# Talking-heads attention and squared-ReLU FFN: the first batch's triple matrices, loads and w_out are rearranged

## The chip, the cores and the metric

The kernel runs on one core of a Trainium2 chip. The core has a matrix engine (TensorE, PE in the profile; PEld is its weight load), three engines for elementwise work (VectorE = DVE, ScalarE = ACT, GpSimd = POOL), SyncE (SP), which here only issues DMAs, and 16 DMA engines that all queues share. Loads from memory are issued by POOL and go through one queue (the page's q0); copies inside the core and stores are issued by SP and go through another (q1). The metric is the device time of one execution in microseconds.

## The reference

```python
scores = scale * np.matmul(q, k.transpose(0, 1, 3, 2))        # 8 batches, 12 heads, 448 x 448, head_dim 64
scores = np.einsum('bhij,hg->bgij', scores, w_pre)            # mix over the heads
scores = scores - np.max(scores, axis=-1, keepdims=True)
attn = np.exp(scores)
attn = attn / (np.sum(attn, axis=-1, keepdims=True) + 1e-09)
attn = np.einsum('bhij,hg->bgij', attn, w_post)               # mix over the heads again
attn_out = np.matmul(attn, v)
x = attn_out.transpose(0, 2, 1, 3).reshape(3584, 768)
h = np.maximum(x @ w_in, 0.0)                                 # w_in 768 x 2048
out = h * h @ w_out                                           # w_out 2048 x 768
```

Inputs and output are float32; inside, the kernel works in bfloat16 with float32 sums.

## The kernel before, in words

**One batch.** k and q are loaded with a cast to bfloat16 and transposed: for the first two batches on PE (L481), later by DMA transposes that SP issues (L557, L563), after POOL or DVE has copied them into place (L544). The 448 query rows of a head are 128 x 3 = 384 rows in three blocks (r = 1, 2, 3) and a tail of 64 rows (r = 0), for which the q of two heads are laid side by side (qt, transposed into zt). `score` (L607) makes the scores of a block, one matmul a head (L619), and DVE or ACT copies them into snat, one of two buffers, rows on partitions (L385 for DVE, L387 for ACT).

**Relayout.** The mixing over heads needs heads on partitions. `relayout` (L654) therefore copies pieces of snat by DMA into a tile sch of 120 partitions (10 query rows x 12 heads) and 448 keys; there are 11 such buffers. A batch has 45 such chunks. `move` (L647) issues the DMA on SP (L648). A buffer of snat may be written again when all relayouts that read it have landed.

**Chunk.** `chunk` does, for each piece: mixing by w_pre on PE (L743), minimum on DVE (L748, mn; the sign is turned), exponential with its sum on ACT (L751, es), reciprocal on DVE (L757, rc), the product with w_post on POOL (L760, wq), the second mixing on PE (L767), and a copy on DVE or ACT into atb (L385, L387). Six of these can be under way. `av` multiplies atb by v (L807) into xt.

**The first batch's triples.** In the first batch, the tail (r = 0) and the first block (r = 1) are moved by six large relayouts instead, of 120 rows x 1,344 elements: each serves three chunks, and such a chunk is made by three matmuls (L739) with masked copies of the mixing matrix. These 18 matrices of 120 x 120 are in one tile, wtri_all. `spread` (L429) makes six products of 120 x 120 on PE, three to a bank (L431); `thin` (L435) writes each of them three times, masked by a column of keep_m, on DVE (L438) or ACT (L440): 18 evictions. The relayouts' targets are osb (three times) and h2 (three times, "h" in the profile).

**FFN.** `unit` takes 128 or 256 rows of xt through w_in (L860), ReLU on ACT (L873, hr), the square on POOL (L876, h), w_out (L892), a copy on DVE (L907, osb) and a store (L916).

**Loads.** The first batch's k, q and tails are loaded at the start. Behind them POOL issues three pieces of w_in, two halves of v, and the other three pieces of w_in (`first_batch`, L1007; `load_w1`, `load_v`). The four pieces of w_out (`load_w2`, L982) are issued at steps 18, 21, 24 and 27 of the first batch, each 512 rows of w_out by all 768 columns. The loads of the second batch are issued at steps 13 and 16.

**What sets the order.** All instructions are written into fixed orders by a planner, a small list scheduler that runs when the kernel is built (`Planner.run`, L117). Every operation has an engine (or two to choose from), a duration and a priority (mostly the number of the chunk, with an offset such as AHEAD = 7 chunks for relayouts and scores). DMAs are modelled as two queues, LOAD and DMA, with a cost per row alone and a cost when both are active (`moved`, `settle`). The planner's durations only choose orders; on the chip an instruction waits for semaphores, and on each engine the order is kept.

## Time and profile before

| | us |
|---|---|
| median of 3 runs (597.18 to 598.89) | 597.46 |
| profiled execution, whole time | 597.42 |
| profiled execution, span | 595.6 |
| PE busy, 95% of the span | 565.2 |
| DVE busy, 81% | 484.6 |
| ACT busy, 80% | 475.9 |
| POOL busy, 55% | 325.0 |

The page's second part shows the span in 40 equal slices, each digit the busy share of a slice in tenths. In the timeline a row gives an instruction's start and duration, its engine, line, what it writes and reads, and in brackets how long the engine was idle before it and who ended that. Merged rows carry a count (x6). A row of the stretches gives, for PE, PEld, DVE, ACT and POOL, the busy time and the count of instructions, then the granted share of PE's clock, the mean busy share of the DMA engines (it can pass 1 where packets overlap) and the GB/s moved.

### The profile page before, as it was taken

The page shows a single profiled execution, that of the slowest core. Times are in us where ns is not written, and L with a number is a line of the kernel's source. Part 1 is how long each engine was busy: PE and PEld are TensorE (multiplying, and loading weights), DVE is VectorE, ACT ScalarE, POOL GpSimd, SP SyncE. Part 2 cuts the span into 40 slices and gives each one's busy share as a digit, 9 for nine tenths or more (in the row PEclk, how much of TensorE's full clock was granted, in tenths as well). Part 3 has the DMA queues.
Part 4 walks back from the last instruction along what each step waited for, and adds up shares of the span by engine and source line. Part 5 has one row for each costly group of instructions (what it writes and reads, how often), then busy time and mean ns, then how long its engine had stood idle before and what let it go on. Part 6 is the DMA issues. An engine that isn't in the chain of part 4 may idle for free.

```text
span 595.6 us, 17018 instructions
## 1 busy us (share of the span) xinstructions
PE 565.2 (95%) x5751; PEld 402.4 (68%) x5751; DVE 484.6 (81%) x1248; ACT 475.9 (80%) x1246; POOL 325.0 (55%) x596
## 2 busy tenths in 40 slices
PE   4687978999999999999999999999999999999996
PEld 2345765587667766776866868776867767777873
DVE  5699958989989898999799998989799998888011
ACT  4488967898888898998898978888888888998420
POOL 8026635564567637753784728653884726445530
PEclk9799999999999999999999999999999999999999
DMA  9959963986499647974399649884398646322011
GB/s 136 234 125 175 220 144 83 197 177 146 103 162 177 151 120 136 187 172 135 94 179 173 157 114 164 173 146 133 87 191 165 150 116 126 119 82 69 2 53 54
DMA packets 130038, 82.33 MB, mean 138 GB/s; under 512 B 59582, under 2 KB 124238, under 8 KB 129950
## 3 DMA queue, kind: packets, MB, share of 16 engines
q1 hardware_dynamic: 85214, 58.42, 38.7%
q0 software_dynamic: 44736, 22.81, 29.4%
q8 instruction: 45, 0.74, 0.5%
q14 instruction: 43, 0.35, 0.2%
HBM read 45.62 MB, written 11.01 MB: 95 GB/s over the span
## 4 chain that ended last, share of the span: by engine, by line
PE 84%; DVE 6%; DMA 4%; issue 2%; ACT 2%; POOL 1%; SPq 0%; DVEq 0%; ACTq 0%; POOLq 0%
PE bank L892 24%; PE bank L860 24%; PE bank L767 12%; PE bank L743 11%; PE bank L807 6%; PE bank L619 6%; DVE mn L748 2%; DMA sch<-snat 2%; DVE atb L385 1%; DMA osb<-snat 1%; DVE snat L385 1%; PE bank L739 1%; DMA ks<-in_k_dram 1%; ACT es L751 1%; DVE rc L757 1%
## 5 line engine op out<-in xcount | busy, mean ns | idle before, releaser
L751 ACT ACTIVATE es<-bank,mn 120x448 bf16<-120x448 f32 x360 | 229.5, 644 | 37.0 <-DVE mn L748 27.3
L760 POOL TENSOR_SCALAR wq<-wback,rc 120x120 bf16<-120x120 f32 x360 | 132.2, 371 | 196.5 <-DVE rc L757 113.9
L748 DVE TENSOR_REDUCE mn<-bank 120x1 f32<-120x448 f32 x360 | 210.2, 609 | 7.8 <-PE bank L739 5.3
L892 PE MATMUL bank<-w,h 128*128 128x384 bf16 x896 | 173.9, 325 | 0.6 <-DVE osb L907 0.3
L860 PE MATMUL bank<-xt,w 128*128 128x256 bf16 (+1 forms) x1632 | 165.5, 255 | 0.0
L385 DVE CAST atb<-bank 112x480 bf16<-112x480 f32 (+2 forms) x222 | 135.1, 620 | 23.5 <-PE bank L767 21.3
L860 PEld LDWEIGHTS <-w 128*128 128x128 bf16 x1632 | 137.3, 98 | 22.5 <-issue 2.0
L876 POOL TENSOR_TENSOR h<-hr 128x512 bf16<-128x512 f32 x112 | 116.6, 1041 | 57.3 <-ACT hr L873 57.1
L767 PEld LDWEIGHTS <-es 120*112 120x112 bf16 (+1 forms) x1440 | 113.2, 130 | 41.1 <-issue 11.3
L767 PE MATMUL bank<-wq,es 120*112 120x120 bf16 (+1 forms) x1440 | 124.9, 217 | 7.6 <-POOL wq L760 5.9
L892 PEld LDWEIGHTS <-h 128*128 128x128 bf16 x896 | 84.0, 97 | 54.8 <-issue 4.9
L385 DVE CAST snat<-bank 128x448 bf16<-128x448 f32 x170 | 98.8, 611 | 11.9 <-DMA sch<-snat 5.3
L743 PE MATMUL bank<-sch,wmix 120*128 120x448 bf16 x334 | 105.3, 354 | 0.1
L387 ACT CAST atb<-bank 112x480 bf16<-112x480 f32 (+2 forms) x162 | 88.2, 555 | 11.4 <-PE bank L767 10.5
L873 ACT ACTIVATE hr<-bank 128x512 f32<-128x512 f32 x112 | 67.0, 599 | 33.3 <-PE bank L860 28.9
L387 ACT CAST snat<-bank 128x448 bf16<-128x448 f32 x166 | 82.7, 546 | 11.2 <-DMA sch<-snat 4.4
L751 ACT ACTIVATION_READ_ACCUMULATOR es<-bank,mn 120x1 f32 x360 | 75.8, 211 | 0.0
L757 DVE RECIPROCAL rc<-sm 120x1 f32<-120x1 f32 x360 | 52.9, 153 | 20.3 <-ACT es L751 16.6
L907 DVE COPY osb<-bank 128x384 f32<-128x384 f32 x56 | 30.9, 551 | 35.9 <-PE bank L892 35.8
L619 PE MATMUL bank<-kt,qz 64*128 64x448 bf16 x288 | 43.3, 359 | 4.9 <-DVE snat L385 3.8
L743 PEld LDWEIGHTS <-wmix 120*128 120x128 bf16 x342 | 29.9, 98 | 18.6 <-issue 11.1
L807 PE MATMUL bank<-atb,vs 112*64 112x192 bf16 (+3 forms) x864 | 40.4, 250 | 0.2
(56 smaller groups left out, 250.8 us busy)
## 6 DMA issues: line engine op xcount, KB each, us to landing
sch<-snat SPq DMA_DIRECT2D x318, 105.0 KB
out_dram<-osb SPq DMA_DIRECT2D x23, 360.0 KB
vs<-in_v_dram POOLq DMA_DIRECT2D x16, 336.0 KB, 9.4
ks<-in_k_dram POOLq DMA_DIRECT2D x14, 336.0 KB, 7.0
qs<-in_q_dram POOLq DMA_DIRECT2D x14, 288.0 KB, 7.1
w<-in_moe_w_in_dram POOLq DMA_DIRECT2D x6, 512.0 KB, 14.7
w<-in_moe_w_out_dram POOLq DMA_DIRECT2D x4, 768.0 KB, 19.7
out_dram<-osb SPq DMA_DIRECT2D x8, 192.0 KB
```

The source lines that it names most:

```text
L385: nc.vector.tensor_copy(out=out_, in_=in_)
L387: nc.scalar.copy(out=out_, in_=in_)
L619: nc.tensor.matmul(slot[:, 0:S], lhsT=lhsT, rhs=kt[i][half, :, at_, :], start=True, stop=True)
L743: nc.tensor.matmul(slot[:, 0:S], lhsT=wm[0:rows, :], rhs=src[0:rows, :], start=True, stop=True,)
L748: nc.vector.tensor_reduce(out=mn[i][0:rows, :], in_=slots[mk][0:rows, 0:S], axis=AX.X, op=ALU.min)
L751: nc.scalar.activation(out=es[i][0:rows, 0:S], in_=slots[mk][0:rows, 0:S], func=ACT.Exp, scale=-1.0, bias=mn[i][0:rows, 0:1], accum_out=sm ...
L760: nc.gpsimd.tensor_scalar(out=wq[i][0:rows, :, 0:ns], in0=wback[0:rows, :, 0:ns], scalar1=rc[i][0:rows, 0:1], scalar2=1.0, op0=ALU.mult, o ...
L767: nc.tensor.matmul(slot[0:P_KEYS, jb * H * ns:(jb + 1) * H * ns], lhsT=es[i][0:rows, jb * P_KEYS:(jb + 1) * P_KEYS], rhs=wq[i][0:rows, :, ...
L807: nc.tensor.matmul(v_[64 * hh:64 * hh + 64, i, 0:x1 - x0], lhsT=vs[:, 2 * c2 + hh, jb, :], rhs=atb[half][:, jb, 2 * c2 + hh, x0:x1], start ...
L860: nc.tensor.matmul(slot[:, j * w:(j + 1) * w], lhsT=w1[c2][:, (f0 + j) * 128:(f0 + j + 1) * 128], rhs=xt[:, c2, a:z], start=(c2 == 0), sto ...
L876: nc.gpsimd.tensor_tensor(out=h2_[:, f0:f0 + nf, 0:w], in0=hr[gi % 2][:, :].rearrange("p (f c) -> p f c", f=nf), in1=hr[gi % 2][:, :].rear ...
L892: nc.tensor.matmul(slot[:, 0:384], lhsT=h2_[:, ft, mt * 128:(mt + 1) * 128], rhs=w2[:, ft, nt * 384:(nt + 1) * 384], start=(ft == 0), stop ...
```

## The change

- The evictions into wtri_all take three products at a time (120 x 3 x 120): six instructions instead of 18.
- v and w_in of the first batch are loaded behind a small copy on POOL (hold), which reads snat after all scores of the first batch's tail have been copied there; v comes first, then the six pieces of w_in.
- A piece of w_out is now 1,024 rows by half of the columns (384) instead of 512 rows by all 768. Size, number and steps of the loads stay.
- In the planner, a relayout that finds its queue empty while a load is in progress is held until up to 50 rows of loads have passed (FIFO); the loads' costs alone and beside other traffic are set apart, with new numbers (also for q, k and the tails, in `first`, `load_tails` and `load_ahead`); AHEAD goes from 7 to 7.4. This emits no instruction and changes orders.

```diff
-AHEAD = 7
+AHEAD = 7.4
+FIFO = 50
@@ class Queue
+        self.last, self.wait = -1, -1
@@ Planner.run
                 if eng in queues:
                     x = queues[eng]
+                    y = queues["LOAD"]
+                    if eng == "DMA" and x.op is None and heap and y.op is not None and x.last != t and x.wait < t:
+                        ahead = max(0.0, y.left - (t - y.at) * y.rate) + sum(z[2].rows[0] for z in ready["LOAD"])
+                        x.wait = t + int(min(ahead, FIFO) * y.op.rows[1])
+                        heapq.heappush(events, (x.wait, n, None))
+                        n += 1
+                    if eng == "DMA" and x.wait > t:
+                        continue
...
@@ load
-        done = pl.moved("LOAD", rows, each, each, 0, [op], 1500)
+        done = pl.moved("LOAD", rows, each[0], each[1], 0, [op], 1500)
@@ thin
-    def thin(eng, tail, m, x):
-        src, to = slots["g", "tri", tail][0:KC, x * KC:(x + 1) * KC], wtri[3 * tail + m][x][:, 0:KC]
+    def thin(eng, tail, m):
+        src = slots["g", "tri", tail][0:KC, 0:3 * KC].rearrange("p (x k) -> p x k", x=3)
+        to = wtri_all[:, 9 * tail + 3 * m:9 * tail + 3 * m + 3, 0:KC]
...
         for m in range(3):
-            for x in range(3):
-                thins.append(add(
-                    {"DVE": 220, "ACT": 300}, 0, at_pri + 0.1 * m, lambda eng, tail=tail, m=m, x=x: thin(eng, tail, m, x), [mm],
-                ))
-                tri_ready.setdefault(3 * tail + m, []).append(thins[-1])
+            thins.append(add(
+                {"DVE": 500, "ACT": 560}, 0, at_pri + 0.1 * m, lambda eng, tail=tail, m=m: thin(eng, tail, m), [mm],
+            ))
+            tri_ready.setdefault(3 * tail + m, []).append(thins[-1])
@@ load_w1, load_w2, load_half
-        w1_in.append(load(16, 173, pri, lambda: nc.gpsimd.dma_start(
+        w1_in.append(load(16, (152, 148), pri, lambda: nc.gpsimd.dma_start(
...
     def load_w2(f4, n):
-        done = load(32, 135, n, lambda: nc.gpsimd.dma_start(
-            out=w2[:, 4 * f4:4 * f4 + 4, :],
-            in_=moe_w_out[512 * f4:512 * f4 + 512, 0:DMODEL].rearrange("(f p) c -> p f c", p=128),
+        f_, c_ = 8 * (f4 % 2), 384 * (f4 // 2)
+        done = load(64, (62, 79), n, lambda: nc.gpsimd.dma_start(
+            out=w2[:, f_:f_ + 8, c_:c_ + 384],
+            in_=moe_w_out[128 * f_:128 * f_ + 1024, c_:c_ + 384].rearrange("(f p) c -> p f c", p=128),
         ), gate(n))
...
+    def load_half(b, n, x, deps):
+        h0 = x * H // 2
+        v_in[b].append(load(42, (46, 58), n, lambda: load_kv(vs, v, b, h0, h0 + H // 2), deps))
@@ load_v
-        v_in[b] = [load(42, 60, n, lambda h0=h0: load_kv(vs, v, b, h0, h0 + H // 2), deps) for h0 in (0, H // 2)]
+        v_in[b] = [load(42, (46, 58), n, lambda h0=h0: load_kv(vs, v, b, h0, h0 + H // 2), deps) for h0 in (0, H // 2)]
...
@@ first_batch
         for i in range(NPAIR):
-            if i == LAST_W1:
-                load_v(0, 0.1 + i, [started])
-            load_w1(i, 0.1 + i)
...
         for r in (1, 0):
             for p in groups(0, r):
                 score(0, r, p)
+        hold = sb.tile([P, NPAIR], BF16, name="hold")
+        opened = add("POOL", 150, -6, lambda: nc.gpsimd.tensor_copy(
+            out=hold[:, :], in_=store_of(0, 0)[:, 0:NPAIR, 0],
+        ), scopy[0, 0])
+        for x in range(0, 2):
+            load_half(0, -5 + 0.1 * x, x, [opened])
+        for i in range(NPAIR):
+            load_w1(i, -4 + 0.1 * i, [opened])
```

More of the change, by code (lines that the diff above doesn't have):

```diff
@@ L75 @@
 Q1_AT = [13, 16]
-LAST_W1 = 3
+LAST_W1 = 4
 TAIL0, Q0 = 19, 0.7
@@ L234, in run @@
                         done.ns = t - done.at
-                        x.op = None
+                        x.op, x.last = None, t
                         x.turn += 1
@@ L946, in first @@
     def first(us, rows, each):
-        return pl.moved("LOAD", rows, each, each, 0, [add("FIRST", 0, us, lambda: None, lat=1000 * us + 1600)], 1500)
+        return pl.moved("LOAD", rows, each, each, 0, [add("FIRST", 0, us, lambda: None, lat=1000 * us + 1600)], 1300)
     at_, tails0 = 1.3, []
@@ L951 @@
         if what == "k":
-            k_in[0, x] = first(at_, 28, 60)
+            k_in[0, x] = first(at_, 28, 48)
         elif what == "q":
-            q_in[0, x] = first(at_, 32, 52)
+            q_in[0, x] = first(at_, 32, 36)
         else:
-            tails0.append(first(at_, 24, 32))
+            tails0.append(first(at_, 24, 24))
         at_ += 1.1 if at_ < 2 else 0.75
@@ L975, with load_w1 @@
     w2_in = [add("W2", 0, 0, lambda: None, lat=0) for i in range(4)]
-    def load_w1(c2, pri):
-        w1_in.append(load(16, 173, pri, lambda: nc.gpsimd.dma_start(
+    def load_w1(c2, pri, more=()):
+        w1_in.append(load(16, (152, 148), pri, lambda: nc.gpsimd.dma_start(
             out=w1[c2][:, :], in_=moe_w_in[c2 * 128:(c2 + 1) * 128, 0:DFF], max_dma_last_dim=4096,
-        ), [started]))
+        ), [started, *more]))
     def load_w2(f4, n):
-        done = load(32, 135, n, lambda: nc.gpsimd.dma_start(
-            out=w2[:, 4 * f4:4 * f4 + 4, :],
-            in_=moe_w_out[512 * f4:512 * f4 + 512, 0:DMODEL].rearrange("(f p) c -> p f c", p=128),
+        f_, c_ = 8 * (f4 % 2), 384 * (f4 // 2)
+        done = load(64, (62, 79), n, lambda: nc.gpsimd.dma_start(
+            out=w2[:, f_:f_ + 8, c_:c_ + 384],
+            in_=moe_w_out[128 * f_:128 * f_ + 1024, c_:c_ + 384].rearrange("(f p) c -> p f c", p=128),
         ), gate(n))
@@ L988, in load_w2 @@
         w2_in[f4].left += 1
+    def load_half(b, n, x, deps):
+        h0 = x * H // 2
+        v_in[b].append(load(42, (46, 58), n, lambda: load_kv(vs, v, b, h0, h0 + H // 2), deps))
     def load_v(b, n, deps):
-        v_in[b] = [load(42, 60, n, lambda h0=h0: load_kv(vs, v, b, h0, h0 + H // 2), deps) for h0 in (0, H // 2)]
+        v_in[b] = [load(42, (46, 58), n, lambda h0=h0: load_kv(vs, v, b, h0, h0 + H // 2), deps) for h0 in (0, H // 2)]
     def load_tails(b, n, deps):
-        tails = [load(24, 32, n, lambda x=x: load_tail(b, x), deps) for x in range(2)]
+        tails = [load(24, (24, 32), n, lambda x=x: load_tail(b, x), deps) for x in range(2)]
         tail_in[b] = add("TAIL", 0, n, lambda: None, tails, lat=1000 if b else 0)
@@ L999, in load_ahead @@
         got = [
-            load(48, 52, n, lambda: load_q(b, g0, g0 + 6), wars + gate(n)),
-            load(42, 60, n, lambda: load_kv(ks, k, b, g0, g0 + 6), wars + gate(n)),
+            load(48, (36, 52), n, lambda: load_q(b, g0, g0 + 6), wars + gate(n)),
+            load(42, (46, 58), n, lambda: load_kv(ks, k, b, g0, g0 + 6), wars + gate(n)),
         ]
@@ L1008, in first_batch @@
         for i in range(NPAIR):
-            if i == LAST_W1:
-                load_v(0, 0.1 + i, [started])
-            load_w1(i, 0.1 + i)
+            if i == 0:
+                v_in[0] = []
+                for x in range(0):
+                    load_half(0, -30 + x, x, [started])
         for p in range(NPAIR):
```

## The prediction

> **What bounds the kernel now.** I read the page first: busy shares, then the rows of 40 slices (one slice is 14.9 us).
>
> ```profile
> span 595.6 us, 17018 instructions
> ...
> PE   4687978999999999999999999999999999999996
> ...
> DVE  5699958989989898999799998989799998888011
> ...
> PEclk9799999999999999999999999999999999999999
> DMA  9959963986499647974399649884398646322011
> ```
>
> From slice 8 on PE is full. Adding up the gaps between PE's instructions gives 25.8 us of idle PE, 24.3 of them before 100 us (5.5 before the first matmul) and 1.5 after. Whatever is saved before 100 us moves the end one for one; what comes later can hardly be sped up.
>
> Then the timeline of the first 60 us, which shows the first hole and what stands before it. Columns: start, duration, engine, line, what, and in brackets the idle time and who ended it.
>
> ```profile
> 7.41 0.34 DVE L438 TENSOR_SCALAR wtri_all<-bank,keep_m 120x120 bf16<-120x120 f32 x1 [0.35 <-ACT wtri_all L440]
> 7.78 0.36 ACT L440 ACTIVATE wtri_all<-bank,keep_m 120x120 bf16<-120x120 f32 x1 [0.41 <-DVE wtri_all L438]
> ...
> 17.31 1.82 SPq L648 DMA_DIRECT2D osb<-snat  x2
> ...
> 21.84 2.66 SPq L648 DMA_DIRECT2D h<-snat  x3
> 24.44 5.22 PE L739 MATMUL bank<-osb,wtri_all 120*128 120x448 bf16 x15 [3.73 <-DMA osb<-snat]
> ```
>
> The 18 evictions into wtri_all take turns on DVE and ACT, each waiting for the other. The first triple relayout is issued at 17.31, and PE stands still until 24.44. Then the timeline of 74 to 92 us, the second hole:
>
> ```profile
> 85.52 1.16 DVE L385 CAST snat<-bank 128x448 bf16<-128x448 f32 x2 [4.82 <-DMA sch<-snat]
> 86.20 0.88 PE L619 MATMUL bank<-kt,qz 64*128 64x448 bf16 x4 [3.27 <-DVE snat L385]
> ...
> 87.82 2.75 PE L860 MATMUL bank<-xt,w 128*128 128x128 bf16 x24
> ```
>
> DVE and ACT are free from 80.7, but may not overwrite snat until the last relayout of the first batch has read it. Last, stretches of 2 us (busy time and count of PE, PEld, DVE, ACT, POOL; granted clock, DMA share, GB/s):
>
> ```profile
> 22.00:24.00 2.00, 0.00 (x0) 0.00 (x0) 0.00 (x0) 0.00 (x0) 0.00 (x0) 0.54 1.18 292
> 24.00:26.00 2.00, 1.56 (x5) 0.65 (x5) 0.24 (x1) 0.00 (x0) 0.00 (x0) 0.50 1.25 233
> ```
>
> After each hole PE runs at half clock: 6.83 us from 22.16, and 3.41 us from 87.02.
>
> The trace's DMA packets tell why the holes are there; loads go in the software queue, relayouts in SP's, on the same 16 engines. (a) osb's 2,688-byte packets start at 21.60, 4.3 us after the issue; a relayout into idle queues (schl, issued 42.74) starts after 1.4. In the missing 2.9 us about 50 packets of loads per engine go by (42 of v, the rest w_in). So a relayout that finds its own queue empty and loads ahead waits behind some 50 of these. (b) From 65 to 83.5 us every relayout of 120 packets takes 2.05 us (1.95 to 2.1), though all that count were issued by 69.4. The rate of w_out fits ten engines that take one 1,536-byte and one 896-byte packet in turn: 12 pairs of 171 ns.
>
> **The change, part by part.** The sum is against the profiled execution, 597.42 us (span 595.6); the median of the runs is 597.46.
>
> Evictions. 18 of 120 columns (ten at about 0.30 to 0.34 on DVE, eight at 0.36 on ACT: 6.1 us, taking turns from 7.0 to 14.2) become six of 360 columns. Not in the trace; between 0.34 (120 columns) and 0.61 (448) on DVE, 0.36 and 0.55 on ACT, by columns 0.53 and 0.50. The planned order gives DVE three in a row, then ACT three: 3.1 us and one handover. What this frees comes from the new order of PE: 7.67 start of the tails' transposes, 0.8; two zt copies on ACT to 9.2; then score 0.4, spread 0.5, k transposes 1.0, score 0.4, k transposes 1.0, two scores 0.7, q transposes 0.85, two scores 0.7, copy 0.6 = 15.3, less overlap of about 0.3: the six tails' copies are done at 15.0, against 17.2.
>
> Loads. The tensor_copy to hold on POOL (bounds: 0.10 for a 128x1 memset, 0.61 for a 112x512 copy; I take 0.2, near the 0.25 of the 120x144 memset) waits for those copies at 15.0; behind it on POOL stand 2 issues of v (0.78) and 6 of w_in (0.73) = 5.9 us, to 21.1, then the first wq. POOL was idle from 14.1 to 29.0, and six es buffers let ACT run six chunks without wq, so this costs nothing; without that cover the first wq, due at about 21.5, would be late by what the issues run over. The issues pass no other on POOL, but on the engines they now come behind osb's two relayouts instead of ahead: osb0 starts at 15.0 + 1.4 = 16.4, v at 15.2 + 1.6 (first k load: issued 1.30, first packet 2.94) = 16.8. osb0 takes 1.75 beside v, as it did before (21.60 to 23.35), and PE started 1.1 after its last packet: first chunk at 19.3, 5.1 earlier, and with less than the 3.7 us of idle PE that took the clock away.
>
> The next wait is for h. Its relayouts need all twelve copies of the next scores: after 14.7 some 14 snat copies of 0.58, four qz of 0.4 and 0.45 of wmix are left for two engines: about 19.5. They reach the engines at 20.9, when osb and schl are through (20.2). By (a) h0 then waits behind 50 packets, all of v at 51 ns (21 per engine in 1.08 us): 2.6. Beside w_in it takes 2.3 (26.29 to 28.58), plus 1.1: 26.9 for chunk 7, which ran at 30.70. Front: -3.8. Ends: no wait, then ACT's pace (six es at 0.83) sets 25.3, -5.4; or 50 packets of w_in at 156 ns, 32.1, +1.4. The first is nearer to the row of osb; I take -3.8.
>
> What is late next: v is in by 25 (needed 54.8 - 3.8), w_in by about 43 (96 packets per engine, 32 of them paired at 290 ns, 64 at 156, from 23.5) against its first use at 58.05 - 3.8. The relayouts of the third block, issued 38.9 instead of 42.7, meet its last 15 packets (2.4 us); their rows are used 5.4 (schl) and 7.1 us (sch) after the issue, so I count 0, at most +1.
>
> w_out. Four issues as before, at the same steps, but of 1,024 packets of 768 bytes instead of 512 of 1,536. A relayout beside packets of 384 and 512 bytes took 0.8 to 1.2 (55.0 to 63.4), beside 1,536 it takes 2.05; by bytes, from 1.1 at 512, that is 1.34 at 768. 9.8 relayouts stand before the hole at 63.4: 13.1 instead of 20.0 us, so the last lands 6.9 earlier, 78.6 against DVE's 80.7. The hole goes: 3.27 of idle PE and half of 3.41 at half clock = -5.0. Ends: 0 (the packet's cost is not its bytes) and -6.5 (DVE's 4.8 plus the slow stretch). w_out itself takes no longer: 256 packets per engine, most paired at 112 ns, is 28 us, as now (57.1 to 86.0); PE first needs it at 96.95, so some 10 us could be lost there before it shows.
>
> AHEAD 7.4, the new costs and the hold on lone relayouts emit nothing; they change orders. Before the 46th chunk both orders put 192 w_in matmuls and 60 scores, so PE's filling is the same. In the later batches SP's transposes and stores move past one to three relayouts each. PE idles 1.5 us there, so it can lose more than win: +0.5 (-1 to +4).
>
> [...]
>
> Sum: 597.4 - 3.8 - 5.0 + 0.5 = 589.1.
>
> **Rivals.** No lone wait for h0: SP's queue is not dry when h0 comes, or it waits for one packet only; 587.5. For it: h0 did follow osb within 1.1 us at 25.2. Against it: (a), and a second such wait of 2.2 us at 48 us. Front eaten: h0 meets w_in, or v's first packets arrive before osb0's (0.4 apart): front +0.5, second hole gone, 593. Speed of relayouts unchanged at 768 bytes: the hole stays, 594. Against it the 0.8 to 1.2 beside 512. Nothing gained: both at once, about 597.5. Slower: SP is in order, and in the six later batches the transposes of k and q now stand ahead of two relayouts more; if POOL's copies for them come late, the relayouts behind wait too, and PE with them, once per batch, at the price of the hole at 82.9 (5.0 with its clock). Two such stalls eat the gain, three give 604. Against it: seven or more chunks of relayouts are in hand, and the order before loses 1.5 us in all.
>
> **How the numbers follow.** Forecast 0.48 (own range 587 to 591.5); no lone wait 0.13; front eaten 0.14; relayouts no faster 0.08; nothing gained 0.05; slower 0.12. Within 0.3% (1.8 us) is about what a measurement can't tell from no change. Faster 0.83, same 0.05, slower 0.12. The range 585.5 to 595.5 leaves out the last two cases and a little more.
>
> **What would show it.** First triple matmul at 19 to 20 us; no half clock at 22 to 29; three evictions in a row on each engine; chunk 7 at about 27; relayouts of about 1.3 us between 58 and 80; no DVE wait near 80 for a relayout; PE idle before 100 us down from 24.3 to about 15, and still under 2 after. Wrong if h's first packets start after 25, if relayouts stay at 2 us, or if PE has new holes after 100 us.

## The result, and the profile after

The changed kernel takes 591.25 us (median of 4 runs, 589.72 to 591.78) against 597.88 us (597.18 to 598.89) for the kernel before: a ratio of 0.9884, 95% interval 0.987 to 0.9898. The forecast was 589.1 us with a range of 585.5 to 595.5. The gain is 6.6 us where 8.4 were forecast. The profiled execution took 591.14 us, with a span of 589.4.

The page of the kernel after, in 40 slices of 14.7 us:

```profile
span 589.4 us, 17018 instructions
...
PE   5698999999999999999999999999999999999996
...
DVE  4697999997798998999898898989798898989201
...
PEclk9897999999999999999999999999999999999999
DMA  8899969984596449964596639974497547322021
```

Compare the digits with those of before. DVE's sixth slice goes from 5 to 9: the hole beside w_out is gone. But its fourth slice goes from 9 to 7, and the clock's 7 has moved from the second slice to the fourth: something new stands at 44 to 59 us.

The timeline of the front, with its evictions, its first relayouts and the first triple matmuls:

```profile
8.88 0.59 DVE L449 TENSOR_SCALAR wtri_all<-bank,keep_m 120x360 bf16<-120x360 f32 x1 [2.92 <-PE bank L441]
9.51 1.01 ACT L451 ACTIVATE wtri_all<-bank,keep_m 120x360 bf16<-120x360 f32 x2 [0.39 <-DVE wtri_all L449]
10.11 1.09 DVE L449 TENSOR_SCALAR wtri_all<-bank,keep_m 120x360 bf16<-120x360 f32 x2 [0.63 <-ACT wtri_all L451]
11.23 0.56 ACT L451 ACTIVATE wtri_all<-bank,keep_m 120x360 bf16<-120x360 f32 x1 [0.71 <-DVE wtri_all L449]
...
15.15 1.82 SPq L658 DMA_DIRECT2D osb<-snat  x2
...
15.70 1.59 POOL L330 DMA_DIRECT2D vs<-in_v_dram  x2 [0.30 <-issue]
...
19.56 1.86 PE L749 MATMUL bank<-osb,wtri_all 120*128 120x448 bf16 x9 [2.15 <-DMA osb<-snat]
...
24.33 1.19 PE L749 MATMUL bank<-osb,wtri_all 120*128 120x448 bf16 x3 [2.91 <-DMA osb<-snat]
```

Up to 19.56 the times are near the forecast (tails' copies done at 15.0, first triple at 19.3). Then PE waits a second time for osb: the second relayout's 120 packets run from 19.06 to 23.7 us, 4.6 instead of 1.75. The two engines still take turns on wtri_all, each waiting 0.4 to 0.7 for the other, but with six evictions there are three such handovers.

The third block, first as stretches of 2 us (columns as in the stretches of before), then in the timeline:

```profile
44.00:46.00 2.00, 1.49 (x10) 0.60 (x9) 2.00 (x6) 1.96 (x6) 2.00 (x4) 1.00 0.91 218
46.00:48.00 2.00, 1.15 (x10) 0.75 (x10) 2.00 (x7) 1.88 (x5) 2.00 (x6) 1.00 1.28 225
48.00:50.00 2.00, 1.50 (x12) 0.90 (x12) 2.00 (x4) 1.28 (x3) 1.97 (x4) 0.59 1.36 187
50.00:52.00 2.00, 1.59 (x10) 0.90 (x9) 2.00 (x9) 1.34 (x4) 1.41 (x3) 0.50 1.37 199
52.00:54.00 2.00, 2.00 (x39) 1.91 (x39) 0.55 (x2) 0.91 (x3) 1.29 (x2) 0.50 1.48 213
```

```profile
46.29 0.35 PE L753 MATMUL bank<-schl,wmix 96*128 96x448 bf16 x1 [0.69 <-DVE snat L395]
...
49.34 0.56 PE L753 MATMUL bank<-sch,wmix 120*128 120x448 bf16 x1 [0.50 <-DMA sch<-snat]
...
51.33 0.55 PE L753 MATMUL bank<-sch,wmix 120*128 120x448 bf16 x1 [0.41 <-DMA sch<-snat]
...
52.17 2.77 PE L817 MATMUL bank<-atb,vs 112*64 112x128 bf16 x48
```

This hole is new. None of its waits is above 0.7 us, but half clock begins at 48.37, for 6.83 us; the 48 matmuls with v then take 2.77 us (1.53 for 48 of the same shape at full clock, at 72.92), and meanwhile DVE is busy for 0.55 us of 2. Mind the order: in the 3.41 us in front of 48.37 PE stood for 1.36 us, 0.69 of them for a copy into snat on DVE (the first row) and none above 0.3 besides; its two waits for relayouts (0.50 and 0.41) come after the clock had gone.

And the stretch where the second hole stood:

```profile
78.20 1.15 DVE L395 CAST snat<-bank 128x448 bf16<-128x448 f32 x2
80.00 0.11 PEld L629 LDWEIGHTS <-qz 64*128 64x128 bf16 x4
80.00 0.55 PE L629 MATMUL bank<-kt,qz 64*128 64x448 bf16 x4
```

The scores that came at 86.20 after a wait of 3.27 come at 80.00, and the copies into snat wait for nothing.

**One account for all kernels.** For every kernel below I added up, from PE's rows, what PE loses: its idle time, and half of its busy time at half clock (an estimate: by the 2.77 and 1.53 us above it would be 45%). PE's end less this sum lies between 558.4 and 561.2 us for all fourteen kernels, so most of what differs is in these two terms, and a difference of 1 or 2 us in the sum is not all seen in the time. Each row is one execution, the profiled one; other executions of the same kernel can have another granted clock (with the loads behind osb 0.982 in the profiled one, 0.987 to 0.99 in the other five). By stretches of the span (idle + half clock, us):

| kernel | ratio to before (95%) | 0-40 | 40-70 | 70-100 | behind 100 |
|---|---|---|---|---|---|
| before | | 14.1+2.3 | 4.2+0 | 6.0+1.7 | 1.4 |
| after | 0.9884 (0.987-0.9898) | 12.8+1.7 | 2.8+3.0 | 2.0+0 | 1.9 |
| after, w_out in rows | 1.0007 (0.9987-1.0027) | 12.5+1.6 | 2.6+3.0 | 6.0+1.6 | 2.2 |
| before, w_out in columns | 0.9942 (0.9926-0.9958) | 15.4+3.0 | 2.2+1.6 | 3.4+0 | 1.3 |
| after, 18 evictions | 0.9913 (0.9896-0.993) | 13.3+2.8 | 3.1+3.1 | 2.1+0 | 2.0 |
| after, old loads, planned anew | 1.0012 (0.9994-1.0029) | 13.9+3.1 | 2.6+4.6 | 2.7+1.7 | 4.6 |
| after, old loads, same order | 0.9900 (0.9886-0.9915) | 13.5+2.3 | 3.9+0 | 2.0+1.7 | 2.2 |
| after, v first, planned anew | 1.0013 (0.9998-1.0028) | 14.6+2.6 | 4.0+1.7 | 3.4+0 | 3.6 |
| after, old planner | 1.0081 (1.0047-1.0116) | 14.2+1.8 | 4.7+4.1 | 4.0+1.7 | 6.1 |
| after, w_in later | 0.9882 (0.9867-0.9897) | 12.2+2.2 | 2.5+3.1 | 2.0+0 | 2.1 |
| after, w_in's first piece early | 0.9920 (0.9903-0.9936) | 11.7+4.3 | 3.1+3.3 | 2.1+0 | 2.1 |
| after, v and w_in behind the 2nd wq | 0.9917 (0.9891-0.9943) | 14.0+2.8 | 3.6+3.1 | 2.1+0 | 2.5 |
| after, second batch's loads early | 0.9876 (0.9835-0.9916) | 12.7+1.7 | 2.8+3.0 | 2.0+3.3 | 1.8 |
| after, loads behind osb | 0.9893 (0.987-0.9915) | 10.9+1.7 | 4.3+3.6 | 2.0+3.3 | 2.0 |

From before to after: front -1.9, 40 to 70 us +1.6, 70 to 100 us -5.7, behind it +0.5. This adds up to -5.5; PE's end came 6.2 earlier.

### The profile page after: what moved, and what is told of

It is laid out like the page before. It is cut to its first block, busy times and chain, and to the rows that moved or that the text cites. A ratio compares the mean times of both kernels' runs of the same rounds, so it can differ in the third digit from the quotient of the medians.

```text
span 589.4 us, 17018 instructions
## 1 busy us (share of the span) xinstructions
PE 565.2 (96%) x5751; PEld 403.8 (69%) x5751; DVE 486.1 (82%) x1240; ACT 471.3 (80%) x1239; POOL 326.2 (55%) x600
## 4 chain that ended last, share of the span: by engine, by line
PE 84%; ACT 5%; DMA 5%; issue 2%; DVE 1%; SPq 1%; POOL 1%; DVEq 0%; POOLq 0%; ACTq 0%
PE bank L902 24%; PE bank L870 24%; PE bank L777 12%; PE bank L753 10%; PE bank L817 7%; PE bank L629 6%; DMA sch<-snat 3%; ACT es L761 2%; DMA osb<-snat 1%; SPq L658 1%; ACT snat L397 1%; ACT hr L883 1%; DVE mn L758 1%; PE bank L491 1%; DMA qt<-in_q_dram 1%
## 5 line engine op out<-in xcount | busy, mean ns | idle before, releaser
L770 POOL TENSOR_SCALAR wq<-wback,rc 120x120 bf16<-120x120 f32 x360 | 130.5, 367 | 179.4 <-DVE rc L767 104.2
L395 DVE CAST atb<-bank 112x480 bf16<-112x480 f32 (+3 forms) x227 | 142.1, 634 | 30.8 <-PE bank L777 27.8
L870 PEld LDWEIGHTS <-w 128*128 128x128 bf16 x1632 | 135.7, 98 | 21.9 <-issue 2.3
L777 PEld LDWEIGHTS <-es 120*112 120x112 bf16 (+1 forms) x1440 | 116.9, 130 | 39.5 <-issue 8.1
L777 PE MATMUL bank<-wq,es 120*112 120x120 bf16 (+1 forms) x1440 | 129.6, 218 | 2.8 <-POOL wq L770 1.9
L753 PE MATMUL bank<-sch,wmix 120*128 120x448 bf16 x334 | 103.9, 355 | 1.3 <-DMA sch<-snat 0.9
L395 DVE CAST snat<-bank 128x448 bf16<-128x448 f32 x164 | 96.0, 612 | 6.3 <-PE bank L629 3.5
L397 ACT CAST atb<-bank 112x480 bf16<-112x480 f32 (+3 forms) x157 | 82.3, 540 | 15.7 <-PE bank L777 14.2
L397 ACT CAST snat<-bank 128x448 bf16<-128x448 f32 x172 | 84.9, 550 | 4.3 <-PE bank L629 3.2
L817 PE MATMUL bank<-atb,vs 112*64 112x192 bf16 (+3 forms) x864 | 42.2, 255 | 0.5 <-ACT atb L397 0.5
```

What stands on the lines that cost most here:

```text
L395: nc.vector.tensor_copy(out=out_, in_=in_)
L397: nc.scalar.copy(out=out_, in_=in_)
L753: nc.tensor.matmul(slot[:, 0:S], lhsT=wm[0:rows, :], rhs=src[0:rows, :], start=True, stop=True,)
L770: nc.gpsimd.tensor_scalar(out=wq[i][0:rows, :, 0:ns], in0=wback[0:rows, :, 0:ns], scalar1=rc[i][0:rows, 0:1], scalar2=1.0, op0=ALU.mult, o ...
L777: nc.tensor.matmul(slot[0:P_KEYS, jb * H * ns:(jb + 1) * H * ns], lhsT=es[i][0:rows, jb * P_KEYS:(jb + 1) * P_KEYS], rhs=wq[i][0:rows, :, ...
L817: nc.tensor.matmul(v_[64 * hh:64 * hh + 64, i, 0:x1 - x0], lhsT=vs[:, 2 * c2 + hh, jb, :], rhs=atb[half][:, jb, 2 * c2 + hh, x0:x1], start ...
```

## The experiments

### w_out: columns taken back, and columns alone

The changed kernel with w_out's old pieces (all else the same, the planned order too):

```diff
-            out=w2[:, f_:f_ + 8, c_:c_ + 384],
-            in_=moe_w_out[128 * f_:128 * f_ + 1024, c_:c_ + 384].rearrange("(f p) c -> p f c", p=128),
+            out=w2[:, 4 * f4:4 * f4 + 4, :],
+            in_=moe_w_out[512 * f4:512 * f4 + 512, 0:DMODEL].rearrange("(f p) c -> p f c", p=128),
```

> The changed kernel with w_out loaded in rows again (512 rows by 768 columns, 1,536-byte packets); every engine keeps the order of the changed kernel, only these four DMAs have the old shape. Theory (small packets let the relayouts through): relayouts take 2.05 us again between about 58 and 78 instead of 1.26 to 1.4, the last of the first batch lands some 6 us later, DVE and ACT wait 3 to 5 us for it near 77, PE idles about 3 us and runs 3.4 us at half clock after it: 595 to 596.5. Rival (the hole is gone because the planner ordered the work around it): relayouts may be slow, but no wait near 77 to 82 and a time within 1 us of the changed kernel's 591.3.

Measured: 598.21 us (596.1 to 599.69), ratio 1.0007 (0.9987 to 1.0027). The timeline of this kernel where the copies into snat wait:

```profile
81.14 1.16 DVE L395 CAST snat<-bank 128x448 bf16<-128x448 f32 x2 [4.96 <-DMA sch<-snat]
81.67 1.03 PE L629 MATMUL bank<-kt,qz 64*128 64x448 bf16 x4 [2.74 <-ACT snat L397]
```

The hole is back with all it had: DVE waits 4.96 us for a relayout, PE 2.74 for DVE and ACT, and 3.41 us of half clock follow at 83.4. By the packets, relayouts of 120 packets take 1.97 to 2.1 us each between 65 and 75 us, from the start of the first packet to the start of the last (1.24 to 1.38 in the changed kernel). In the account only the column of 70 to 100 us differs, by 5.6.

The other way round, the kernel before with w_out in columns and nothing else (the same lines with the signs turned, f_ and c_ as in the change):

> The kernel before with w_out loaded in halves of columns, all orders as before: this part alone. Theory (small packets): relayouts of 1.3 to 1.4 us from 65 us on instead of 2.05, the wait of DVE at 80.7 to 85.5 goes, and with it 3.3 us of idle PE and 3.4 us of half clock: 592.5 to 594. Rival (the planner's order is needed): 597 to 598, the wait stays.

Measured: 593.91 us (593.39 to 594.48), ratio 0.9942 (0.9926 to 0.9958). Its timeline at the same scores:

```profile
82.71 1.16 DVE L385 CAST snat<-bank 128x448 bf16<-128x448 f32 x2 [0.26 <-PE bank L619]
84.61 0.11 PEld L619 LDWEIGHTS <-qz 64*128 64x128 bf16 x4
84.61 0.55 PE L619 MATMUL bank<-kt,qz 64*128 64x448 bf16 x4
```

The hole is gone (-4.3 in the account), and relayouts beside w_out take 1.05 to 1.4 us. So the shape of w_out's packets made the hole. It is worth 3.7 us in the old order and some 7 us in the new one. All other parts together, without it, gain nothing that can be measured.

### The evictions

Each of the six evictions written as three of 120 columns, on the same engine, at the same place:

```diff
     def thin(eng, tail, m):
-        src = slots["g", "tri", tail][0:KC, 0:3 * KC].rearrange("p (x k) -> p x k", x=3)
-        to = wtri_all[:, 9 * tail + 3 * m:9 * tail + 3 * m + 3, 0:KC]
+        for x in range(3):
+            thin_one(eng, tail, m, x)
...
```

> The changed kernel with each of the six evictions written as three of 120 columns, on the same engine and at the same place; every other instruction keeps its place. Theory A (the evictions lie on the way to the tails' copies): three of 0.30 to 0.36 us instead of one of 0.55 to 0.59 add 0.42 us three times on each engine, 1.3 us; the tails' copies are done at about 16.3 instead of 15.05, the first triple matmul comes at 20.8, and all that follows is 1.3 us later: 592.5 us (592 to 593). Theory B (the copies wait for PE's scores, not for the evictions): first triple at 19.6 and 591.3 us (590.8 to 591.8).

Measured: 592.76 us (591.33 to 593.35), ratio 0.9913 (0.9896 to 0.993). In its timeline, the evictions and what follows:

```profile
10.80 1.60 DVE L452 TENSOR_SCALAR wtri_all<-bank,keep_m 120x120 bf16<-120x120 f32 x6 [0.93 <-ACT wtri_all L454]
12.43 0.87 ACT L454 ACTIVATE wtri_all<-bank,keep_m 120x120 bf16<-120x120 f32 x3 [0.91 <-DVE wtri_all L452]
...
16.05 1.83 SPq L661 DMA_DIRECT2D osb<-snat  x2
```

osb's first relayout is issued 0.9 us later, and the front loses 1.7 us in the account. The time is 1.5 us above that of the changed kernel, as theory A has it, though the two intervals overlap a little (0.9896 to 0.9898). The evictions do lie on the way to the copies.

### The place of the loads

First, the loads at their old place and no copy to hold, with the order of the instructions planned for this:

```diff
-            if i == 0:
-                v_in[0] = []
-                for x in range(0):
-                    load_half(0, -30 + x, x, [started])
+            if i == 3:
+                load_v(0, 0.1 + i, [started])
+            load_w1(i, 0.1 + i)
...
-        hold = sb.tile([P, NPAIR], BF16, name="hold")
...
```

> The changed kernel with v and w_in issued where they were before (three pieces of w_in, v, three pieces of w_in, right behind the first loads; no hold copy); the planner orders anew. Theory A (loads behind the scores win the front): osb0 waits behind 50 packets again, first triple matmul at about 22.3 instead of 19.6, and the time is 1 to 3 us worse, 592.5 to 594. Theory B (what they win at the first matrix they lose at the second, at 21.4 to 24.3, and again at 48 to 55, where the third block's relayouts stand behind the end of w_in): fourth chunk at about 24.3 and seventh at about 27.5, as early as in the changed kernel, w_in through at about 36 instead of 48, no half clock at 48 to 55, and 588.5 to 590.5.

Measured: 597.86 us (596.57 to 600.32), ratio 1.0012 (0.9994 to 1.0029). Both theories missed. The front is as one would think: osb's first packet comes at 18.36, 4.4 us behind its issue, and PE is at half clock for 10.24 us from 17.82 on. But the kernel also loses 4.6 us behind 100 us, where no load of the first batch is left, and 2.4 more at 70 to 100 us. So this run tells little about the place of the loads; the whole order was another.

Then v alone in front, right behind the first loads, and w_in behind the copy to hold, planned anew as well:

```diff
-                for x in range(0):
+                for x in range(2):
...
-        for x in range(0, 2):
+        for x in range(2, 2):
```

> The changed kernel with v loaded right behind the first loads, where the DMA engines stood idle from 12.8 to 16.7; w_in stays behind the hold copy. Theory (v's packets and their late end are what costs): v runs from about 11.5 to 15, osb1 lands by about 21 instead of 23.7 and its wait of 2.9 us goes, w_in is through at about 45, the half clock at 48 to 55 shrinks: 589 to 590. Rival (osb1 is slow because POOL writes descriptors at the same time, whatever it loads): osb1 lands at 23 to 24 as now, and the time is within 1 us of 591.3.

Measured: 598.58 us (597.15 to 600.42), ratio 1.0013 (0.9998 to 1.0028). osb's second relayout is no faster without v beside it: it starts at 21.59, 3.1 us behind the end of the first, while w_in's first packets pass, and lands at 24.74. Here too 3.6 us are lost behind 100 us.

Because of these two, all later kernels but one keep every instruction at its place and move only POOL's issues. The old place once more, in the changed kernel's order:

```diff
-    started = add("POOL", int(1000 * at_) + 700, -100, lambda: None)
+    def old_place():
+        for i in range(NPAIR):
+            if i == 3:
+                for h0 in (0, H // 2):
+                    load_kv(vs, v, 0, h0, h0 + H // 2)
+            put_w1(i)
+
+    started = add("POOL", int(1000 * at_) + 700, -100, old_place)
...
```

> The changed kernel with w_in and v issued by POOL at their old place (behind the first loads); the copy to hold stays, and every other instruction of every engine keeps its place, which the first run with the old loads did not. Theory A (the loads' new place wins in front and gives it back at 45 to 55 us): osb's first packet comes about 3 us late behind w_in, chunk 7 at about 29, some 10 us of half clock in front, but w_in is in before 38, the gap at 45.6 and the half clock from 48.4 go: +0.8 + 3.4 - 1.4 - 3.4, so 590.6 us (589.5 to 592). Theory B (the loads' place is worth the whole gain, as the run with the old loads and its own order has it): 597 to 598.5 us.

Measured: 591.79 us (591.38 to 592.25), ratio 0.99 (0.9886 to 0.9915). Theory A holds. From its timeline, the front and the third block:

```profile
14.85 1.82 SPq L658 DMA_DIRECT2D osb<-snat  x2
...
22.71 5.27 PE L749 MATMUL bank<-osb,wtri_all 120*128 120x448 bf16 x15 [5.60 <-DMA osb<-snat]
...
47.30 0.35 PE L753 MATMUL bank<-schl,wmix 96*128 96x448 bf16 x1 [0.69 <-DVE snat L395]
...
50.91 0.37 PE L777 MATMUL bank<-wq,es 120*112 120x120 bf16 x4 [1.44 <-POOL wq L770]
```

osb waits behind w_in (first packet at 19.63) and the front is 1.4 us worse than in the changed kernel; but w_in is in at 39.4, the third block's first relayout starts 1.43 us behind its issue, and 40 to 70 us is 1.9 us better. That is the clock's doing alone: idle PE is 1.1 us more there than in the changed kernel, with a wait of 1.44 us for wq, but no half clock came. At 88.8 it has 3.41 us of half clock that the changed kernel has not. The new place of the loads wins in front about what it loses in the third block; the two times differ by 0.5 us and their intervals overlap. Of the 1.0012 of the first run, what is not in 0.99 came with the order.

### The planner's part

AHEAD back at 7, no hold on relayouts, the old costs of the loads; evictions, loads and columns stay:

```diff
-AHEAD = 7.4
-FIFO = 50
+AHEAD = 7
+FIFO = 0
...
-                    y = queues["LOAD"]
-                    if eng == "DMA" and x.op is None and heap and y.op is not None and x.last != t and x.wait < t:
...
-        w1_in.append(load(16, (152, 148), pri, lambda: nc.gpsimd.dma_start(
+        w1_in.append(load(16, (173, 173), pri, lambda: nc.gpsimd.dma_start(
```

> The changed kernel with the planner's part undone: AHEAD 7, no hold on relayouts, the loads' old costs. Evictions, the place of the loads and w_out in columns stay; the order of the instructions is planned anew. Theory A (the new costs buy an order that is worth several us: the two runs whose order was planned anew lost 6 to 7 us, while the old place of the loads in the changed kernel's own order lost 0.5): 594 to 597.5 us. Theory B (the planner's part is worth nothing, or half a us the other way, as forecast): 590 to 592 us.

Measured: 602.21 us (601.96 to 604.4), ratio 1.0081 (1.0047 to 1.0116): slower than the kernel before, and by more than theory A gave it. It loses in every stretch against the changed kernel: 1.5, 3.0, 3.7, and 4.2 us behind 100 us, where nothing but the order differs. PE's waits behind 100 us in this kernel (who waits, for whom, us in total, times, longest):

```profile
PE bank L621 <- DVE snat L387: 1.3, 1, 1.3
PE bank L769 <- POOL wq L762: 1.2, 3, 0.6
PE bank L769 <- ACT es L753: 1.1, 4, 0.4
```

and in the changed kernel:

```profile
PE bank L902 <- ACT es L761: 0.5, 1, 0.5
PE bank L777 <- ACT es L761: 0.3, 1, 0.3
```

The kernel before was planned with just these old costs and loses 1.4 us behind 100 us. So they are not bad as such: they give a good order for the old kernel and a bad one for the new. Three kernels whose order was planned anew for another first batch lose 3.6, 4.6 and 6.1 us behind 100 us; the two in the order of before and the nine in the changed kernel's order lose 1.3 to 2.5. Which of AHEAD, the hold and the costs carries it was not tried.

### What makes osb's second relayout slow

w_in's six issues moved behind the second wq, v's left where they are:

```diff
         def f_wq():
...
+            if n == 1:
+                for c2 in range(NPAIR):
+                    put_w1(c2)
...
```

> The changed kernel with the six issues of w_in moved behind the second wq on POOL (from 17.3 to about 23 us); v stays. What made osb's second relayout take 4.6 us? Theory A (POOL's issuing of w_in and its descriptors): osb's second relayout takes 1.75 to 2.2 us, chunk 4 starts by 22.5 and chunk 7 by 26; w_in lands some 2 us later than 48.1, the wait at 45.6 grows by 1 to 2: 589.5 to 592 us. Theory B (v's 512-byte packets beside it): osb's second relayout still takes 4 us or more, chunk 4 at 24.3, chunk 7 at 28, and with w_in later 592 to 594 us.

Measured: 590.51 us (590.1 to 591.71), ratio 0.9882 (0.9867 to 0.9897), the same as the changed kernel. osb's second relayout still runs from 18.33 to 22.88, 4.55 us, and POOL issues w_in only from 22.77 on: theory A's cause is out. B's time was too high; this execution's front started 0.6 us earlier, and w_in landed at 47.2, no later than before.

Then v's issues moved there too:

```diff
+            if n == 1:
+                for h0 in (0, H // 2):
+                    load_kv(vs, v, 0, h0, h0 + H // 2)
+                for c2 in range(NPAIR):
+                    put_w1(c2)
...
```

> The changed kernel with v and w_in both issued behind the second wq on POOL (at about 22 us instead of 15.7 to 21.6), all else at its place. Theory A (v's first packets beside osb's second relayout make it take 4.4 to 4.6 us): without them both relayouts take 1.6 to 2 us, chunk 4 comes at about 21.5 and chunk 7 at 24.5 to 26, no gap above 1.5 us in front; w_in lands at 50 to 51 instead of 48.1 and the third block gives 1 to 2 us back: 589 to 591.5 us. Theory B (osb's second relayout is slow of itself, by what it reads or writes): it takes 4 us or more here too, chunk 4 at 24, and with w_in later the time is 592 to 594 us.

Measured: 593.85 us (593.19 to 594.16), ratio 0.9917 (0.9891 to 0.9943). Its front in the timeline:

```profile
19.18 3.00 PE L749 MATMUL bank<-osb,wtri_all 120*128 120x448 bf16 x15 [1.77 <-DMA osb<-snat]
...
24.23 4.33 POOL L993 DMA_DIRECT2D w<-in_moe_w_in_dram  x6
28.55 1.08 POOL L770 TENSOR_SCALAR wq<-wback,rc 120x120 bf16<-120x120 f32 x3
29.03 0.56 PE L782 MATMUL bank<-wq,es 120*112 120x120 bf16 x4 [4.93 <-POOL wq L770]
```

Without a load beside them osb's relayouts take 1.73 and 1.46 us, and chunk 7 comes at 23.37 instead of 28.14. So theory A is right about the cause: osb's second relayout is slow because v starts beside it. That any first packets do this is not shown: in the two kernels with the old loads v's come straight behind those of w_in, and the relayouts of osb that start beside them take 1.7 to 2.1 us. But the time is 2 to 2.6 us above that of the changed kernel, and the last row says why: the third wq stands behind eight issues on POOL, and PE waits 4.93 us for it. That is the price of the cover named in the prediction (POOL idle while the loads are issued), once it is gone.

Last, the loads behind osb but out of wq's way: the copy to hold reads the first block's scores, v and two pieces of w_in are issued behind it, the rest one by one between the next wq:

```diff
+            if n == 0:
+                nc.gpsimd.tensor_copy(out=holds[0][:, :], in_=store_of(0, 1)[:, H - NPAIR:H, 0])
+                for h0 in (0, H // 2):
+                    load_kv(vs, v, 0, h0, h0 + H // 2)
+                put_w1(0)
+                put_w1(1)
...
+            if n in (1, 2, 3, 4):
+                put_w1(n + 1)
...
```

> The changed kernel with the loads 3.5 us later, but out of wq's way: the copy to hold reads the first block's scores instead of the tail's (it is then released with h's first relayout, at about 18.7), v and two pieces of w_in are issued behind it, and the other four pieces singly behind the second to the fifth wq. Theory A (the slow relayout is the one that v's first packets meet, and only a wq behind a row of issues cost the run before its gain): osb's two relayouts take 1.5 to 1.8 us each, h's take the loss, chunk 4 at 21, chunk 7 by 26.5 instead of 28.1, chunk 8 without a wait for wq; w_in lands 2 us later and the third block gives 1 us back: 589.5 to 590.7 us. Theory B (the loss only moves on to h's relayouts, and w_in's delay weighs more): chunk 7 at 27.5 or later, 591.3 to 593.5 us.

Measured: 592.21 us (589.4 to 592.92), ratio 0.9893 (0.987 to 0.9915). The front does what theory A says, and the time what B says. In the timeline:

```profile
24.27 0.73 PE L749 MATMUL bank<-h,wtri_all 120*128 120x448 bf16 x3
...
46.98 0.56 PE L753 MATMUL bank<-sch,wmix 120*128 120x448 bf16 x1 [1.11 <-DMA sch<-snat]
...
49.20 0.56 PE L753 MATMUL bank<-sch,wmix 120*128 120x448 bf16 x1 [1.26 <-DMA sch<-snat]
```

Chunk 7 comes at 24.27, 3.9 us before that of the changed kernel; the slow relayout is now h's second, 22.10 to 25.56, with v's first packets from 21.16 on. The third block comes earlier by as much, while w_in still lands only at 48.5. Its relayouts now run beside w_in all the way, at up to 2.5 us each, PE waits 1.1 to 1.3 us twice, and PE is at half clock for 10.24 us. This clock began at 43.93, ahead of both waits, behind a window with the same 0.69 us for DVE's copy and 0.36 in smaller pieces; the waits come inside it. What the front wins (1.8 us by 40 us, against the changed kernel) is gone at 55 us, and in the profiled execution another 6.83 us of half clock from 88.3 cost 3.3 more.

### What makes the hole at 45 to 55 us

One piece of w_in issued in front, where the DMA engines of the changed kernel stand all but idle (one packet starts between 12.65 and 16.68 us), so that the rest lands earlier:

```diff
-    started = add("POOL", int(1000 * at_) + 700, -100, lambda: None)
+    started = add("POOL", int(1000 * at_) + 700, -100, lambda: put_w1(0))
...
```

> The changed kernel with the first of the six pieces of w_in issued right behind the first loads (before, its packets ran from 12.0 to 14.7 us, ahead of osb's at 16.7); the other five and v stay behind the copy to hold. Theory A (the third block's first relayout waits behind w_in's packets, and this wait makes the gap at 45.6 and the half clock from 48.4): w_in lands at about 42 instead of 48.1, schl's first packet comes at 42 or earlier and the ones behind take about 1 us each, PE has no gap above 0.5 us and no half clock between 45 and 56: 591.25 - 1.4 - 3.4 = 586.5 us (585.5 to 587.5). Theory B (the second batch's loads, issued from 43.5 on, make that gap): it stays, 590.5 to 592 us. Theory C (the early piece delays osb): first triple later by 1 us or more, 592 us or more.

Measured: 592.79 us (591.72 to 593.24), ratio 0.992 (0.9903 to 0.9936). Every step of theory A up to the relayouts came true: w_in lands at 42.4, schl's first packet comes at 40.66, 1.46 us behind its issue, and the next relayouts take 0.6 to 1.2 us each. The hole stays all the same:

```profile
48.39 0.86 POOL L319 DMA_DIRECT2D qs<-in_q_dram  x1
...
49.24 0.78 POOL L330 DMA_DIRECT2D ks<-in_k_dram  x1
50.04 0.38 POOL L770 TENSOR_SCALAR wq<-wback,rc 120x120 bf16<-120x120 f32 x1
...
50.47 0.56 PE L777 MATMUL bank<-wq,es 120*112 120x120 bf16 x4 [1.42 <-POOL wq L770]
```

PE now waits 1.42 us for a wq that stands behind two issues of the second batch's loads, and no packet of a relayout starts between 45.90 and 48.33, when those loads' first packets come. So w_in was not the only cause; that points to the second batch's loads, as theory B has it. The time itself lies where theory C put it, but not for C's reason: the first triple comes at 19.23, no later than in the changed kernel, and what costs is the front's half clock, 10.24 us from 19.71 instead of 3.41. The test of theory B:

```diff
+            if n == 6:
+                load_tail(1, 0)
+                load_tail(1, 1)
+            if n == 8 or n == 13:
+                g0 = 0 if n == 8 else 6
+                load_q(1, g0, g0 + 6)
+                load_kv(ks, k, 1, g0, g0 + 6)
...
```

> The changed kernel with the second batch's six loads of q, k and tails issued 4 to 14 us earlier, in gaps of POOL between two wq (behind the 6th, the 8th and the 13th wq instead of behind the 14th and the 18th); nothing else moves. Theory A (at 43.5 to 46.5 and 47.8 to 49.4 POOL issues loads while five wq are due, PE waits for those, and that leads to the half clock from 48.4): the gaps at 45.6 to 49 shrink by about 1 us and the half clock goes, 586.5 to 589.5 us. Theory B (the third block's relayouts beside w_in make the gap): 590.5 to 592 us; more loads in the queue can even make it longer.

Measured: 591.8 us (588.35 to 592.62), ratio 0.9876 (0.9835 to 0.9916): no difference from the changed kernel that this interval can tell. No wq waits for an issue any more at 43 to 49, yet the half clock from 47.90 is there again, behind 0.69 us for DVE's copy and 0.74 for a relayout beside w_in (a third gap, 0.82, comes at 50.3). In the account 40 to 70 us did not move by 0.1. The 3.3 us of half clock behind 88.86 are those of the profiled execution, the longest of the four (granted clock 0.985; those of 588.35 and 592.28 us had 0.991).

So the hole has no single maker. PE's wait of 0.69 us for DVE's copy stands in all nine kernels of the changed order, also in the one with w_in in by 39.4, and so belongs to the order. On top of it come 0.1 us in each and 0.3 in eight, and then one of two: waits for relayouts beside w_in (0.3 to 0.8 us each, up to 1.3 with the loads behind osb), or 1.4 us for a wq behind the issues of the second batch (with the first packets of its loads against a relayout). Either was found in front of a half clock; in the changed kernel itself it is one wait of 0.28. But the kernel with the old loads in the same order has 1.55 us in one window, 1.44 of them for wq, and kept full clock. What decides is open. Both taken away at once, with the front's gain kept, was not tried.

## Why the prediction was right or wrong

**w_out in columns: right.** -5.0 was forecast, the column of 70 to 100 us moved by -5.7, undoing it costs 5.6 there. A relayout beside 768-byte packets was put at 1.34 us; it took 1.24 to 1.38, the last one 1.6. The last relayout of the first batch was complete at 76.1 (forecast 78.6; 85.2 before), well before DVE's copies at 78.20. The rival by which 768 bytes are no faster is out.

**Evictions: right in effect, the alternation wrong.** 0.58 to 0.59 on DVE and 0.55 to 0.56 on ACT against the 0.53 and 0.50 taken, and the copies done at 15.05 against 15.0. But the rows show three handovers and not one, so that the sum came out right has some luck in it.

**Front: -3.8 forecast, -2.6 at chunk 7 and -1.9 by 40 us.** The mis-sized term is "osb0 takes 1.75 beside v, as it did before", which I used for osb's second relayout too. It took 4.6. The row it came from (21.60 to 23.35) was of a relayout in the middle of v's stream; in the new place it meets v's first packets. As a consequence the forecast "no half clock at 22 to 29" failed: PE stood 2.15 and 2.91 us, and 3.41 us at half clock followed from 24.48. The first triple, at 19.56 against 19.3, is partly luck: the first relayout took 2.41 us and not 1.75 (v's packets came from 17.73 on), but PE started 0.46 us after its last packet and not 1.1. PE's idle time before 100 us fell from 24.3 to 17.6, where about 15 was forecast.

**The wait of h: right time, wrong reason, and not what PE waited for.** h's first relayout was to wait for 50 packets and run from 23.5 to 25.8; it ran from 23.83 to 25.78. It did not wait alone: it came straight behind the slow osb. So the run says nothing on the rival without the wait. Nor did it set chunk 7, as the forecast had it (26.9): PE was busy from 24.33 on with what osb had held up, at half clock up to 27.89, and came to chunk 7 at 28.14 without a wait, 2.4 us after h's last packet.

**The wait of a lone relayout, (a): right that there is one, wrong in its unit.** I counted 50 packets, from one case with v's small ones. The table has this case and ten others, from the relayout's due start (1.43 us behind its issue, or the end of the one ahead) to its first packet:

| relayout | wait, us | load packets per engine in it | KB per engine |
|---|---|---|---|
| before, osb at 21.60 | 2.9 | 45 of 512 B, 4 of 2,048 | 30 |
| old loads, planned anew, osb | 3.0 | 16 of 2,048 | 33 |
| old loads, same order, osb | 3.4 | 15 of 2,048 | 31 |
| v first, osb's second | 3.1 | 13 of 2,048 | 27 |
| after, schl at 42.58 | 2.6 | 15 of 2,048 | 30 |
| 18 evictions, schl | 2.1 | 12 of 2,048 | 25 |
| w_in later, schl | 2.7 | 16 of 2,048 | 33 |
| loads behind 2nd wq, schl | 2.7 | 17 of 2,048 | 34 |
| before, w_out in columns, osb at 22.00 | 3.3 | 55 of 512, 2 of 2,048 | 31 |
| old planner, schl | 2.7 | 41 of 384, 29 of 512 | 30 |
| after, sch at 79.55 | 2.7 | 27 of 768 | 21 |

With packets of 2,048 bytes it is 12 to 17 of them and not 50. The bytes are 25 to 34 KB in ten of the rows, but they are no unit either: the last row, beside w_out, has 21 KB, and ten more kernels with w_out in columns have the same wait there (2.66 to 2.69 us, 27 or 28 packets). The time, 2.1 to 3.4 us, varies least in the table, but the wait at 48 us in the kernel before, beside a load that just begins, is 1.5 by this measure (2.2 in the prediction). What sets it is open. And with w_in's first piece early, schl came when the last piece was all but through, and waited for nothing: its first packet came 1.46 us behind its issue. By these numbers the bound "50 packets of w_in, 32.1" in the forecast was far too long.

**The third block: forecast 0, at most +1; it cost +1.6.** The size of the wait came out, by luck: schl was to be issued at 38.9 and to lose 2.4 us behind the last 15 packets of w_in; it was issued at 38.60 and lost 2.6 behind 15. But these were not the last: 26 per engine were left, for w_in was in at 48.3 and not at 43, and by my own rule schl would have waited for all of them. That the late rows themselves cost next to nothing was right up to 48 us: schl was used 7.7 us after its issue, and just so in the kernel with the old loads in the same order, where it was not late at all. What failed is "so I count 0" for the whole block: the step left out the clock. PE's idle time from 40 to 70 us even fell by 1.4 us, but its small gaps lay so that half clock came, at a price of 3.0. Of the 1.36 us in front of 48.37, 1.07 (0.10, 0.69 and 0.28) stand at the same places in the kernel with the old loads in the same order, which kept full clock. The relayouts behind schl do run beside w_in and the second batch's loads, at up to 1.8 us each, and make PE wait 0.50 and 0.41 us at 49 to 51, inside the half clock.

**Later batches and the planner: +0.5 forecast, +0.5 measured, and still the weakest step.** Behind 100 us PE loses 1.9 instead of 1.4. But I treated the planner's part as something small beside the rest. Undone, it costs 11 us. What I called an order that changes little is, as far as these runs go, an order fitted to this very first batch.

**Rivals.** The outcome is nearest to "front eaten" in mechanism (v's first packets against osb), though it was mostly the second relayout and not the first that they hit, and it cost half of the front and not all of it. The slower side, three stalls in the later batches by SP's order, did not come; with the old planner waits of up to 1.3 us in the later batches did come, and are 4.2 of what that kernel loses.

## What to carry to other kernels

Where an order is planned, a change is not the sum of its parts: undone one at a time they are worth 7 us (columns), about 1.5 (evictions), 0.5 to 1 (loads, within the noise) and 11 (planner), against 6.6 together. To price one part, keep the order and change that part alone; if the order is planned anew, look first at a stretch that the part cannot reach.

A shorter row at the place of a saving is not yet a gain: follow it to the next stretch that shares its resource. Here two ways of bringing chunk 7 forward by another 3.9 and 4.8 us ended 1 us (within the noise) and 2.6 us above the changed kernel: in the one the same load then met the relayouts of the third block and the clock fell twice, in the other its issues stood in wq's way.

A duration taken from a row holds for what ran beside it (here 1.75 us for osb in the middle of v's stream and 4.6 beside v's first packets): ask whether the neighbour was in full stream or just starting.

## What the runs showed of the hardware

- **A load that started could be dear to a copy beside it.** A relayout of 120 packets of 2,688 bytes took 1.1 to 1.75 us alone (eight of them in the two kernels with late loads). Beside a load that was already running it took 1.4 to 2.7, twice 3.1 (the last of the six is left out, for smaller relayouts overlap it). It took 4.4 to 4.7 us where v's first packets came 1.0 to 1.7 us ahead of it through an empty load queue (osb's second in six kernels, the changed one among them), 3.9 in the one with the old planner, and 3.5 in the kernel where h's second met them. Where v followed w_in without a gap, those that started beside v's first packets took 1.7 to 2.1. The DMA engines were not full meanwhile: 94 GB/s and a share of 0.72 between 18 and 20 us in the changed kernel, against 210 GB/s four us later. v's own first 336 packets took 3.4 us there, the next 336 took 1.6. POOL's issuing of w_in is not the cause (4.55 us with w_in issued only from 22.77 on); what it is stays open.
- **A copy that found its own queue empty beside a load started late in eleven cases.** The waits in the table are 2.1 to 3.4 us, with 12 to 70 rows of the load per engine passing, 21 to 34 KB.
- **Half clock came behind small gaps too.** All changes of the clock in a run lie on one grid of 3.41 us (24.48, 27.89, 48.37 and 55.20 in the changed kernel). In the third block half clock began behind windows of that grid in which PE had stood for only 0.9 to 1.8 us (1.36 in the changed kernel, in front of 48.37, where PE was busy for the other 2.05), never in one piece. No bound can be drawn: 1.35 us in the kernel before (window from 49.5), 1.55 in the one with the old loads in the same order (from 47.8), and even 1.91 in one piece in the changed kernel (from 17.65) led to none. At 85 to 89 us the same waits of PE brought half clock where they fell into one window with 1.43 us or more (three kernels), none with 1.25 and 1.40, and none where the grid split them into 0.6 and 1.1 (three kernels); but behind 90 us 1.49 in the kernel before brought none either.
- **With smaller packets of w_out the copies beside it were faster.** A relayout of 120 packets of 896 bytes beside w_out took 1.97 to 2.1 us with packets of 1,536 bytes and 1.24 to 1.38 (the last 1.6) with 768, for the same bytes to load.
